# Decode attention over a long cache: K transposed in place by VectorE, scores by 512-column matmuls, 8 MB loads in three slots

## Chip, cores, metric

One core of a Trainium2 chip. The time is device microseconds (us) of one execution, as the median of several; the profile is one execution taken by the hardware profiler. The single runs of a kernel lie within some 0.2% of each other, and the median of the kernel before was 1311.9 to 1312.1 us in each of the four sets of runs, so differences of 1 us between medians can be read. All runs compared here are in the fast state; each run of an experiment shared its chip with runs of the kernel before. The changed kernel was measured in the first set only (1282.59 us).

## The reference

```python
def _A_ref(x, k_cache, v_cache, wq, wo):     # x (2,1,448); caches (2, 8, 32768, 256) bf16
    q = (x @ wq).reshape(B, Sq, 16, 256).transpose(0, 2, 1, 3)
    k = jnp.repeat(k_cache, 2, axis=1); v = jnp.repeat(v_cache, 2, axis=1)
    scores = jnp.einsum("bhqd,bhkd->bhqk", q, k) * (256 ** -0.5)
    o = jnp.einsum("bhqk,bhkd->bhqd", softmax(scores), v)
    return o.transpose(0, 2, 1, 3).reshape(B, Sq, 16 * 256) @ wo
# ... b = a small MLP with gelu, g = sigmoid((x * gate_w).sum(-1))
return g * a + (1 - g) * b
```

Two batches by 8 K/V heads are 16 groups. Each group has 32,768 positions of 256 values in K and as many in V, 16.8 MB each, so 537 MB must come from HBM for two query rows per group. There is next to no arithmetic per byte: this is a streaming kernel.

## The kernel before

K and V come in tiles of 4 MB (128 partitions, 64 positions each) through a ring of five slots. Each K tile is handled in 16 units. TensorE transposes a unit's eight 128x128 blocks into PSUM, ScalarE and VectorE take turns to copy them to SBUF, and TensorE multiplies each copied block with the two-column q.

```python
R, BR, NB = 64, 4, 5                       # positions per partition and tile, per unit; slots
def T(U):                                  # ... waits for the tile and for the eviction of U - 3
    for i in range(2 * BR):
        r, j = bl * BR + i // 2, i % 2
        e.transpose(bank[:, i * P:(i + 1) * P], kv[:, r, j * P:(j + 1) * P], ident_b[:, :])
def B(U):                                  # scores: K block as weights, q streams (2 columns)
    for i in range(BR):
        for j in range(2):
            e.matmul(pss[:, n, :], buf[:, (2*i+j)*P:(2*i+j+1)*P], qT_sb[:, kvh, j, :, b],
                     start=(j == 0), stop=(j == 1))
def C(v, bl):                              # values: two weights columns, V streams (256 columns)
    e.matmul(ps_o[g % 2][0:2, 0:Dh], pt[:, n, :], kv[:, r, :], start=..., stop=...)
# ... loads, on SyncE, in the order in which they are needed:
for d in seq:
    for pd in before_of[d]:
        E.wait("pe", released(pd))         # the slot's last user
    dma_start(view(d), src)
```

## Time and profile before

| | before |
|---|---|
| median time | 1311.9 us |
| instructions, matmuls | 44,891 and 21,141 |
| moved by DMA | 547.43 MB of data, 2.70 MB of instructions |
| mean rate | 420 GB/s over the span |

The prediction below shows the head of the page, the DMA queues and the stretches. Beside them stand the costliest groups of the page: the line, engine, operation and tiles, the count, busy us and mean ns of one, and the idle time before them with what ended most of it.

```profile
L513 ACT COPY KT<-psT 128x1024 bf16<-128x1024 bf16 x512 | 518.3, 1012 | 702.0 <-PE psT L374 700.2
L515 DVE COPY KT<-psT 128x1024 bf16<-128x1024 bf16 x512 | 354.1, 692 | 835.0 <-PE psT L374 835.0
L374 PE MATMUL psT<-ident_b,ring 128*128 128x128 bf16 x8192 | 556.2, 222 | 41.7 <-DMA ring<-in_A_k_cache_dram 38.3
...
L448 PE MATMUL ps_o<-ring,PT 128*2 128x256 bf16 x3840 | 496.3, 272 | 1.4 <-DMA ring<-in_A_v_cache_dram 1.4
...
L393 PE MATMUL ps_s<-qT_sb,KT 128*128 128x2 bf16 x8192 | 278.4, 163 | 1.2 <-issue 1.2
```

The two eviction groups wait for TensorE for 700 and 835 us, so they bind nothing. TensorE's transposes wait 38.3 us in total for K to land, in a span of 1310: TensorE and DMA are nearly even. The queue names matter later: q1 carries K, V and the weights, q8 and q14 carry instructions.

### The profile page before, as it was taken

What the parts mean: (1) busy time and instruction counts of PE and PEld (TensorE: products, weight loads), DVE (VectorE), ACT (ScalarE), POOL (GpSimd) and SP (SyncE); (2) the same over time, 40 slices, a digit from 0 to 9 for tenths busy, and PEclk for the clock granted to TensorE, in tenths of its full rate; (3) what the DMA queues carried; (4) which work ended last, traced back from release to release, by engine and by line L of the source; (5) the groups of instructions that cost most, each with busy time, mean ns of one, the idle gap of its engine ahead of it and who ended that gap; (6) DMA issues with size and microseconds to landing.
All of it is one profiled execution on the core that took longest, in us unless ns stands there. A gap on an engine that the chain in (4) does not pass through costs nothing.

```text
span 1310.5 us, 44891 instructions
## 1 busy us (share of the span) xinstructions
PE 1234.1 (94%) x21141; PEld 1031.1 (79%) x21141; DVE 388.7 (30%) x641; ACT 538.7 (41%) x597; POOL 1.5 (0%) x10
## 2 busy tenths in 40 slices
PE   4899999999999999999999999999999999999975
PEld 4888888888888787877787877878788778787864
DVE  2243332323332232323223232223232323223210
ACT  3364444444444444444444434444344434444410
POOL 0000000000000000000000000000000000000000
PEclk9699999999999999999999999999999999999986
DMA  9999999999999999999999999999999999999986
GB/s 392 433 424 418 431 428 429 428 426 429 428 430 430 427 430 427 428 430 429 428 428 427 426 423 424 422 429 416 419 420 429 422 428 415 430 423 421 430 344 294
DMA packets 22424, 550.30 MB, mean 420 GB/s; under 512 B 2392, under 2 KB 4576, under 8 KB 4704
## 3 DMA queue, kind: packets, MB, share of 16 engines
q1 hardware_dynamic: 22084, 547.43, 98.1%
q8 instruction: 165, 2.70, 0.8%
q14 instruction: 19, 0.16, 0.0%
q10 hardware_dynamic: 156, 0.01, 0.0%
HBM read 547.43 MB, written 0.00 MB: 418 GB/s over the span
## 4 chain that ended last, share of the span: by engine, by line
PE 53%; DMA 45%; SPq 1%; issue 0%; DVE 0%
DMA ring<-in_A_k_cache_dram 43%; PE psT L374 23%; PE ps_o L448 20%; PE ps_s L393 9%; DMA ring<-in_A_v_cache_dram 3%; SPq L314 0%; SPq L301 0%; PE ps_m L426 0%; PE ps_o L348 0%; PE ps_m L409 0%; PE ps_m L404 0%; PE ps_o L352 0%; PE ps_o L360 0%; PE psT L462 0%; PE ps_o L453 0%
## 5 line engine op out<-in xcount | busy, mean ns | idle before, releaser
L513 ACT COPY KT<-psT 128x1024 bf16<-128x1024 bf16 x512 | 518.3, 1012 | 702.0 <-PE psT L374 700.2
L515 DVE COPY KT<-psT 128x1024 bf16<-128x1024 bf16 x512 | 354.1, 692 | 835.0 <-PE psT L374 835.0
L374 PE MATMUL psT<-ident_b,ring 128*128 128x128 bf16 x8192 | 556.2, 222 | 41.7 <-DMA ring<-in_A_k_cache_dram 38.3
L374 PEld LDWEIGHTS psT<-ident_b,ring 128*128 128x128 bf16 x8192 | 468.0, 99 | 150.5 <-issue 97.7
L448 PE MATMUL ps_o<-ring,PT 128*2 128x256 bf16 x3840 | 496.3, 272 | 1.4 <-DMA ring<-in_A_v_cache_dram 1.4
L448 PEld LDWEIGHTS ps_o<-ring,PT 128*2 128x2 bf16 x3840 | 284.5, 83 | 85.1 <-DMA ring<-in_A_v_cache_dram 1.7
L393 PE MATMUL ps_s<-qT_sb,KT 128*128 128x2 bf16 x8192 | 278.4, 163 | 1.2 <-issue 1.2
L393 PEld LDWEIGHTS ps_s<-qT_sb,KT 128*128 128x128 bf16 x8192 | 259.9, 96 | 0.7 <-issue 0.7
L453 PE MATMUL ps_o<-PT,ring 128*128 128x2 bf16 x512 | 14.1, 164 | 16.9 <-DMA ring<-in_A_v_cache_dram 15.2
L453 PEld LDWEIGHTS ps_o<-PT,ring 128*128 128x128 bf16 x512 | 13.7, 101 | 17.5 <-DMA ring<-in_A_v_cache_dram 15.4
L543 ACT ACTIVATE PT<-ps_s,negm 128x256 bf16<-128x256 f32 x32 | 16.5, 543 | 0.5
L340 PE MATMUL ps_m<-xT,ring 128*128 128x2 bf16 x128 | 3.6, 165 | 9.4 <-DMA ring<-in_A_wq_dram 9.4
L627 DVE TENSOR_SCALAR o_sb<-ps_o,rl 2x256 f32<-2x256 f32 x15 | 7.1, 472 | 16.1 <-PE ps_o L448 16.1
L631 DVE TENSOR_TENSOR attnT<-ps_o,rl 128x2 bf16<-128x2 f32 x2 | 0.2, 158 | 37.9 <-PE ps_o L453 37.9
L604 DVE TENSOR_REDUCE mx<-ps_s 128x2 f32<-128x512 f32 x16 | 10.9, 681 | 1.3 <-PE ps_s L393 1.3
L340 PEld LDWEIGHTS ps_m<-xT,ring 128*128 128x128 bf16 x128 | 3.5, 104 | 9.4 <-issue 9.4
L426 PE MATMUL ps_m<-ident_f,o_sb 2*128 2x2 f32 x60 | 9.4, 258 | 0.6 <-DVE o_sb L627 0.6
L462 PE MATMUL psT<-ring,attnT 128*2 128x448 bf16 x32 | 9.1, 454 | 0.3 <-DVE attnT L631 0.3
L426 PEld LDWEIGHTS ps_m<-ident_f,o_sb 2*128 2x128 f32 x60 | 8.1, 191 | 1.1 <-DVE o_sb L627 0.9
L462 PEld LDWEIGHTS psT<-ring,attnT 128*2 128x2 bf16 x32 | 3.0, 99 | 5.2 <-issue 3.2
L404 PE MATMUL ps_m<-ident_f,mx 128*2 128x128 f32 x32 | 6.1, 272 | 0.0
L409 PE MATMUL ps_m<-diag,ones_f 2*128 2x2 f32 x32 | 6.1, 256 | 0.0
(54 smaller groups left out, 62.1 us busy)
## 6 DMA issues: line engine op xcount, KB each, us to landing
ring<-in_A_k_cache_dram SPq DMA_DIRECT2D x63, 4096.0 KB, 29.5
ring<-in_A_v_cache_dram SPq DMA_DIRECT2D x63, 4096.0 KB, 31.6
ring<-in_A_k_cache_dram SPq DMA_DIRECT2D x4, 1024.0 KB, 16.5
ring<-in_A_v_cache_dram SPq DMA_DIRECT2D x4, 1024.0 KB, 32.4
ring<-in_A_wo_dram SPq DMA_DIRECT2D x1, 3584.0 KB, 30.4
ring<-in_A_wq_dram SPq DMA_DIRECT2D x1, 3072.0 KB, 10.1
ring<-in_B_w_dram SPq DMA_DIRECT2D x1, 1568.0 KB, 35.3
ring<-in_B_w_dram SPq DMA_DIRECT2D x1, 1344.0 KB, 30.7
```

The lines of the kernel that those rows point to most:

```text
L340: E.ins(lambda e, w=w, xk=xk, kc=kc, kvh=kvh, j=j, hh=hh: e.matmul(ps_qT[:, kvh, j, hh, :], w, xk, start=(kc == 0), stop=(kc == KC)), key= ...
L374: E.ins(lambda e, bank=bank, i=i, kv=kv, r=r, j=j: e.transpose(bank[:, i * P:(i + 1) * P], kv[:, r, j * P:(j + 1) * P], ident_b[:, :]), ke ...
L393: E.ins(lambda e, pss=pss, n=n, i=i, j=j, buf=buf, kvh=kvh, b=b: e.matmul(pss[:, n, :], buf[:, (2 * i + j) * P:(2 * i + j + 1) * P], qT_sb ...
L426: E.ins(lambda e, j=j: e.matmul(ps_m[:, C_OT + 2 * j:C_OT + 2 * j + 2], o_sb[g % 2][0:2, j:Dh:2], ident_f[0:2, 0:2], start=True, stop=True ...
L448: E.ins(lambda e, g=g, kv=kv, r=r, n=n, pt=pt: e.matmul(ps_o[g % 2][0:2, 0:Dh], pt[:, n, :], kv[:, r, :], start=(n == 0), stop=(n == NT * ...
L453: E.ins(lambda e, g=g, kv=kv, r=r, n=n, j=j, pt=pt: e.matmul(ps_o[g % 2][:, 2 * j:2 * j + 2], kv[:, r, j:Dh:2], pt[:, n, :], start=(n == 0 ...
L462: E.ins(lambda e, c=c, kvh=kvh, hh=hh, j=j: e.matmul(ps_a, attnT[:, kvh, j, hh, :], wo_v[:, h, j * Dm:(j + 1) * Dm], start=(c == 0), stop= ...
L513: E.ins(lambda e: e.copy(buf[:, :], bank[:, :]), key=("E", U))
L515: E.ins(lambda e: e.tensor_copy(buf[:, :], bank[:, :]), key=("E", U))
L543: E.ins(lambda e, hh=hh: e.activation(PT[g % 2][:, :, hh], ps_s[g % 2][:, :, hh], ACTF.Exp, bias=negm[g % 2][:, hh:hh + 1], scale=SCALE, a ...
L604: E.ins(lambda e: e.tensor_reduce(mx[g % 2][:, :], ps_s[g % 2].rearrange("p n h -> p h n"), AX.X, ALU.max), key=("MX", g))
L627: E.ins(lambda e: e.tensor_scalar(o_sb[g % 2][:, :], ps_o[g % 2][0:2, 0:Dh], rl[g % 2][0:2, 0:1], None, op0=ALU.mult), key=("OS", g))
```

## The change

The intent is to take the transposes and the evictions off TensorE and PSUM. VectorE transposes K where it lies, in 32x32 blocks of 4-byte words (pairs of bf16). The transposed K then streams, 512 columns at a time, past weights in which q stands block-diagonally, and the scores of a whole group gather in one PSUM bank. V streams 512 columns at a time too, past four weight columns, in four column tiles of the array by turns. Loads become 8 MB in three slots.

```diff
-    R = 64
-    BR = 4
+    R = 128
+    CR = 16
-    NB = 5
+    NB = 3
+            def T(idx, blk):                                    # VectorE
+                if blk == 0:
+                    wait_fill(E, ("K", idx))
+                E.ins(lambda e: e.transpose(k_words(idx, blk), k_words(idx, blk)), key=("T", idx, blk))
+            def S(idx):                                         # TensorE, in place of T and B
+                for blk in range(NCK):
+                    E.wait("dve", ("T", idx, blk))
+                    for s in range(NS):
+                        e.matmul(pss, a_win(g, s, k), kv[:, blk * CR:(blk + 1) * CR, s // 2, :, s % 2],
+                                 start=(k == 0 and s == 0), stop=(k == NK - 1 and s == NS - 1))
+            def PV(v):                                          # TensorE, in place of C
+                for kk in range(0, NCK, 2):
+                    for r16 in range(CR):
+                        j = n % 4
+                        e.matmul(ps_o[g % 2][32 * j:32 * j + 4, :], pt[:, r16, k:k + 2, :], rows, ...)
+        for i in range(NTILES + LAG):                           # order of the loads; wo, last V at the end
+            order.append(("K", i)) ... order.append(("V", i - LAG))
+        order += [("WO", 0), ("V", LASTV)]
```

Cut: the weights' places in slot 0, q's copies, the softmax chain (now one maximum per row pair of 128 partial rows), and the last V tile, which comes in five pieces.

## The prediction

> **What bounds the kernel now.** I read the page first: parts 1 and 2, then the DMA queues (part 3), then the chain of waits (part 4).
>
> ```profile
> span 1310.5 us, 44891 instructions
> PE 1234.1 (94%) x21141; PEld 1031.1 (79%) x21141; DVE 388.7 (30%) x641; ACT 538.7 (41%) x597; POOL 1.5 (0%) x10
> ...
> DMA  9999999999999999999999999999999999999986
> ...
> q1 hardware_dynamic: 22084, 547.43, 98.1%
> q8 instruction: 165, 2.70, 0.8%
> ...
> PE 53%; DMA 45%; SPq 1%; issue 0%; DVE 0%
> ```
>
> Two things are full at once: PE is called 94% busy, and the 16 DMA engines are busy 98.1% of the span with the one queue that brings K, V and the weights. The chain names both (PE 53%, DMA 45%), so it doesn't settle which one binds. The table by stretches does. Its columns are the stretch, its length, busy time and instruction count of PE, PEld, DVE, ACT and POOL, the granted clock, the DMA share and GB/s.
>
> ```profile
> 0.00:10.00 10.00, 0.27 (x5) 0.21 (x5) 1.52 (x4) 1.60 (x3) 1.47 (x10) 1.00 0.81 318
> ...
> 200.00:400.00 200.00, 200.00 (x3396) 166.44 (x3393) 63.27 (x103) 88.80 (x100) 0.00 (x0) 1.00 1.00 429
> ...
> 800.00:1000.00 200.00, 192.33 (x3229) 159.59 (x3229) 59.73 (x97) 83.28 (x90) 0.00 (x0) 0.99 1.00 423
> ...
> 1240.00:1260.00 20.00, 20.00 (x304) 15.92 (x303) 5.62 (x11) 7.33 (x12) 0.00 (x0) 1.00 0.93 382
> 1260.00:1280.00 20.00, 10.91 (x196) 9.00 (x193) 0.72 (x4) 0.00 (x0) 0.00 (x0) 0.74 0.84 338
> ...
> 1300.00:1311.00 11.00, 5.26 (x128) 3.71 (x125) 0.90 (x3) 0.00 (x0) 0.00 (x0) 0.50 0.17 69
> ```
>
> From 20 to 1240 us the DMA share is 1.00: no DMA engine is idle. The rate is 423 to 429 GB/s there; the highest of any stretch I asked for was 435 (20 to 40 us). PE could go a little faster than that: in the timeline one pair of units (16 transposes, 16 score matmuls, 8 matmuls with V) repeats every 2.34 us and eats 1.049 MB, which is 448 GB/s. So **DMA binds, with PE some 5% behind it**. DMA loses time only at the two ends: the start, the stretch 1240 to 1280, and the end after the last landing. The DMA queue's own waits and the timeline say why the dip is there:
>
> ```profile
> SPq L314 <- PE ps_o L448: 664.3, 59, 21.1
> SPq L314 <- PE ps_s L393: 525.1, 62, 17.4
> ```
>
> ```profile
> 1253.50 14.51 SPq L314 DMA_DIRECT2D ring<-in_A_v_cache_dram  x2
> ...
> 1268.05 2.78 SPq L301 DMA_DIRECT2D ring<-in_A_v_cache_dram  x4
> ```
>
> The issuing engine waits for slots nearly always, which costs nothing while about three 4 MB loads are under way (29.5 us to landing against some 9.8 us for 4 MB). Near the end, the last V tile is issued only at 1268, when a slot comes free, and the DMA share falls to 0.84.
>
> [...]its packet records show 1213 ns as the median of a 32 KB packet, 27.0 GB/s on one engine, 432 on 16, and 309 ns for 8 KB; from the two, some 8 ns of a packet don't scale with size. [...]
>
> **The change, part by part.**
>
> *PE work removed.* Gone are 8192 transposes, 8192 two-column score matmuls that each load 128 columns, and 3840 V matmuls of 256 columns. They leave for 64 matmuls of 512 columns per 8 MB K tile (32 x 64 = 2048) and 64 of 512 columns per 8 MB V tile (30 x 64 = 1920, plus 2 x 256 = 512 two-column ones for the last group). With some 500 others that is about 5,000 matmuls in place of 21,141. The trace shows 8 V matmuls of 256 columns in 0.96 us, 120 ns each; doubling it, 512 columns should take about 0.22 to 0.24 us: 14 to 15 us per K tile, and 14 to 15 us per V tile if the four column tiles run one after another[...]. A K and a V tile together need 18 to 30 us of PE, against 39.3 us of DMA (16.78 MB at 427 GB/s). PE stops being a near-bound, but as it wasn't the bound, this alone is worth nothing in the middle.
>
> *VectorE work added.* 8 transposes per K tile of 128 x 2048 words: [...]18.3 us per K tile, 584 us in all. VectorE's 512 evictions (page, part 5: 354.1 us) and ScalarE's 512 (518.3 us) go. With softmax and closing work (some 4 us every second pair) VectorE is near 52% busy, inside the 39.3 us of a pair.
>
> *Do three slots of 8 MB feed the queue?* Load n+1 goes into the slot of load n-2 and must be issued before load n has landed, or DMA idles. Load n-2 landed two loads, 2 x 19.6 = 39 us, before load n. A K tile is held 18.3 us of transposes plus the last 8 matmuls, about 20 us. After the second K tile of a group PE must also pass the softmax chain (about 6 us, going by the 1254.7 to 1259.9 us of the timeline) before the V tile, which landed at 19.6, is used: released at 20 + 6 + (5 to 15) = 31 to 41 after the K tile's landing, 11 to 21 us after its own. Both are well below 39. So the queue always has the next load, and the middle stays at DMA's rate. At the start WQ, W1 and W2 share slot 0; K2 needs that slot back, wanted when K1 has landed (24.6 MB, about 57 us), while PE should be done with the weights by about 30 us. Hidden.
>
> *What DMA gains.* (a) The dip at 1240 to 1280: lost there against 427 GB/s are (45 x 20 + 89 x 20) / 427 = 6.3 us; in the packet records 5.1 us of it are idle engines. In the new order wo is issued when V29 is consumed (about 31 us after K31's landing, V30 being under way until 39), and the whole of the last V follows at once. I count 5.5 us won, and 1.5 us of new idling. (b) Instruction fetch: 165 packets of 16 KB at 1.05 us, 10.8 us of each engine's time, and they slow the K packet beside them from 1.2 to about 1.7 us (165 x 0.5 / 16 = 5 us); about 4 us of this overlap, so 11.7 us net. With about a quarter of the instructions left, some 8.5 us are won. (c) Half the completions (2,242 four-byte records, 1.3 us): 0.6 us. (d) If rows of 64 KB go as one packet, 8 ns x 8192 / 16 = 4 us; if split, nothing: 2 us. The start (0.81 share for 10 us) and the end (last landing at 1305.24, 5.3 us before the end: last matmuls, one more product, the store) stay within 0.5 us.
>
> Sum: 1311.9 - 5.5 + 1.5 - 8.5 - 0.6 - 2 - 0.5 = 1296.3; I take **1295 us**, 1.3% faster. The floor: 548 MB at 432 GB/s is 1269, plus 1.8 before the first byte, 5.3 at the end and 1.4 between span and measured time: 1277.
>
> **Rivals.** (1) *VectorE becomes the bound*: if 4-byte words transpose at half the rate, a block takes 4.4 us and a K tile 35. VectorE then does, per two pairs, 70 us of transposes and, in order, the softmax chain and the wait for the V tile that closes a group (20 to 25 us): over 90 against 78.6, some 1500 us. For it: no number for words anywhere in this trace. [...]I give it 5%. (2) *PE's new matmuls run slowly*: the score matmuls read K at a stride of 4 bytes, and PE, waiting in each V tile, may be granted half its clock (the page shows 0.50 to 0.74 in the waiting stretches at the end). At twice the time, K tiles cost 29 and V tiles up to 29: it would show first at wo, which could be issued after V30 has landed, and cost up to 15 us; with everything slow, a few per cent. (3) *All of the DMA losses vanish*: the slow packets (mean 1227 ns against 1213) were PE's and ScalarE's doing, and the rate rises to 431 or more: 1277 to 1285, just past 2%. Against it: they also come in stretches of equal work (429 against 423 GB/s), so they seem to belong to DMA itself. (4) *Nothing moves*: the transfers were hidden anyway, and a gap at each 8 MB hand-over takes back the gain: 1305 to 1312.
>
> **Range and chances.** The gains (a) to (d) are each bounded by a few us, so the middle of the distribution is narrow: 1286 to 1307. Faster by over 2% needs 1285.7 or less, which takes almost the whole of (3): 0.14. Slower needs (1), or (2) in full: 0.06. Within 2%: 0.80.
>
> **What would show it.** Right: DMA share 1.00 from 20 us to about 1290 without the dip; 426 to 431 GB/s; instruction queue below 0.8 MB; VectorE transposes near 2.28 us, 256 of them; VectorE near 50%, ScalarE below 5%; the chain almost all DMA; about 5,000 matmuls. Wrong: transposes over 4 us and DMA shares below 1 in every pair (rival 1); score matmuls over 0.4 us each (rival 2); a middle above 431 GB/s (rival 3); or waits of the issuing engine that end after the load before has landed, with GB/s dips every 20 us.

The 2.28 us for a block is an estimate. The trace of the kernel before has two reductions of 4-byte values on VectorE, 512 a partition in 681 ns (L604) and 128 in 278 (L609): 1.05 ns for each and some 144 ns fixed, by which 2048 would take 2.29 us if the transpose kept that rate, which this trace doesn't show. Nor does it show that the four column tiles overlap; the lower ends of 18 to 30 us and of 5 to 15 us suppose it.

## The result, and the profile after

| | before | after |
|---|---|---|
| median of the runs | 1311.93 us (1311.53 to 1312.07) | 1282.59 us (1282.37 to 1282.84) |
| ratio after to before | | 0.9777, 95% interval 0.9764 to 0.9791 |

A ratio is the mean time of one kernel's fast runs over that of the other's of the same rounds, so it is not quite the ratio of the medians. The change is faster by 2.2%, some 29.4 us; 1295 with a range of 1286 to 1307 was predicted. The direction was right, the size was little more than half of what came, and a gain of over 2% had been given a chance of 0.14 only.

The page of the kernel after, its head, DMA queues and the chain by engine:

```profile
span 1281.1 us, 10758 instructions
...
PE 742.5 (58%) x4977; PEld 306.7 (24%) x4977; DVE 621.8 (49%) x421; ACT 29.0 (2%) x118; POOL 3.5 (0%) x12
...
DMA  9999999999999999999999999999999999999997
...
DMA packets 12780, 548.12 MB, mean 428 GB/s; under 512 B 1336, under 2 KB 3520, under 8 KB 3904
...
q1 hardware_dynamic: 12580, 547.43, 99.1%
q8 instruction: 39, 0.64, 0.2%
...
DMA 60%; DVE 26%; PE 11%; ACT 1%; SPq 1%; issue 0%; another core or an unknown queue 0%; ACTq 0%
```

The data are the same 547.43 MB. Instructions fell to a quarter, the instruction queue q8 from 165 packets to 39, and the packets of data from 22,084 to 12,580. TensorE is at 58%, and 11% of the chain. (The chain also passes through VectorE, 26%, where the release of a slot ends last; but between 20 and 1200 us the packet records show hardly any idle time of the DMA engines, some 0.1 us in the mean of the 16, so nothing is lost there.) The stretches, with the columns that the prediction explains:

```profile
0.00:10.00 10.00, 0.27 (x5) 0.21 (x5) 4.08 (x9) 1.65 (x3) 3.45 (x12) 1.00 0.83 318
200.00:400.00 200.00, 120.04 (x700) 47.50 (x699) 103.09 (x71) 4.93 (x21) 0.00 (x0) 0.76 1.00 434
800.00:1000.00 200.00, 110.71 (x690) 43.65 (x685) 96.68 (x64) 4.92 (x21) 0.00 (x0) 0.78 1.00 433
1220.00:1240.00 20.00, 13.74 (x106) 5.71 (x104) 8.33 (x12) 0.95 (x3) 0.00 (x0) 0.91 0.96 409
1240.00:1260.00 20.00, 11.29 (x268) 8.43 (x269) 0.00 (x0) 0.00 (x0) 0.00 (x0) 0.53 1.01 394
```

The middle rose from 423 to 429 GB/s before to 432 to 434. The share was 1.00 in both kernels there: the engines were hardly ever idle (1.8 us of the 1220 before, in the mean of the 16), and yet they moved less before. The stretch 1220 to 1260 no longer holds a dip like the one of 0.84 and 338 GB/s.

The groups of the page that replace the five shown of before:

```profile
L385 PE MATMUL ps_s<-ring,Abd 128*128 128x512 bf16 x2048 | 529.7, 415 | 435.4 <-DVE ring L604 434.8
L604 DVE STREAM_TRANSPOSE ring<-ring 128x2048 uint32<-128x2048 uint32 x256 | 565.2, 2276 | 418.3 <-DMA ring<-in_A_k_cache_dram 418.3
...
L439 PE MATMUL ps_o<-ring,PT 128*4 128x512 bf16 x1920 | 138.4, 453 | 1.0 <-DMA ring<-in_A_v_cache_dram 1.0
```

VectorE's transpose takes 2276 ns, and 2.28 us had been expected. The mean of 415 ns in the line of the score matmuls is not what one costs, since they overlap: the timeline has eight of them in 1.91 us, 239 ns each. The 64 of a V tile take 3.6 to 6.2 us, down to 57 ns each against the 239: the four column tiles do run beside each other. The waits of the loading engine:

```profile
SPq L311 <- PE ps_s L385: 949.7, 31, 35.8
SPq L311 <- PE ps_o L439: 187.3, 29, 10.8
```

It waits for slots all the time, as before, and as before that costs nothing: V29 was released 29.2 us after K31 had landed (31 was forecast), with V30 still under way for another 10.

Three of the prediction's signs came out otherwise: the middle is above 431 GB/s (its sign of rival 3), the chain is DMA by 60% and not almost all, and the score matmuls show over 0.4 us in the page (its sign of rival 2, a false alarm, as just seen). The first is the one that matters. The question for the experiments is where 29 us came from when 15.6 had been counted.

### The profile page after: what moved, and what is told of

Its sections match the earlier page's. It is cut to its first block, busy times and chain, and to the rows that moved or that the text cites. A ratio compares the mean times of both kernels' runs of the same rounds, so it can differ in the third digit from the quotient of the medians.

```text
span 1281.1 us, 10758 instructions
## 1 busy us (share of the span) xinstructions
PE 742.5 (58%) x4977; PEld 306.7 (24%) x4977; DVE 621.8 (49%) x421; ACT 29.0 (2%) x118; POOL 3.5 (0%) x12
## 3 DMA queue, kind: packets, MB, share of 16 engines
q1 hardware_dynamic: 12580, 547.43, 99.1%
HBM read 547.43 MB, written 0.00 MB: 427 GB/s over the span
## 4 chain that ended last, share of the span: by engine, by line
DMA 60%; DVE 26%; PE 11%; ACT 1%; SPq 1%; issue 0%; another core or an unknown queue 0%; ACTq 0%
DMA ring<-in_A_k_cache_dram 58%; DVE ring L604 23%; PE ps_o L439 7%; PE ps_s L385 2%; DMA ring<-in_A_v_cache_dram 2%; ACT pexp L536 1%; DVE PT L623 1%; DVE mx L609 1%; SPq L306 1%; PE ps_m L406 1%; PE ps_m L396 0%; PE ps_m L401 0%; DVE gmax L611 0%; DVE gmx L617 0%; ACT negm L532 0%
## 5 line engine op out<-in xcount | busy, mean ns | idle before, releaser
L385 PE MATMUL ps_s<-ring,Abd 128*128 128x512 bf16 x2048 | 529.7, 415 | 435.4 <-DVE ring L604 434.8
L604 DVE STREAM_TRANSPOSE ring<-ring 128x2048 uint32<-128x2048 uint32 x256 | 565.2, 2276 | 418.3 <-DMA ring<-in_A_k_cache_dram 418.3
L385 PEld LDWEIGHTS ps_s<-ring,Abd 128*128 128x128 bf16 x2048 | 200.9, 103 | 758.2 <-DVE ring L604 347.3
L439 PE MATMUL ps_o<-ring,PT 128*4 128x512 bf16 x1920 | 138.4, 453 | 1.0 <-DMA ring<-in_A_v_cache_dram 1.0
L439 PEld LDWEIGHTS ps_o<-ring,PT 128*4 128x4 bf16 x1920 | 49.0, 97 | 82.0 <-issue 41.4
L609 DVE TENSOR_REDUCE mx<-ps_s 128x1 f32<-128x512 f32 x16 | 11.1, 692 | 32.2 <-PE ps_s L385 32.2
L415 PE MATMUL ps_m<-sel,o_sb 128*128 128x2 f32 x120 | 16.6, 260 | 12.0 <-DVE o_sb L638 12.0
L623 DVE STREAM_TRANSPOSE PT<-pexp 128x512 bf16<-128x512 bf16 x16 | 11.4, 711 | 23.7 <-ACT pexp L536 23.7
L415 PEld LDWEIGHTS ps_m<-sel,o_sb 128*128 128x128 f32 x120 | 15.3, 196 | 19.6 <-DVE o_sb L638 19.6
L458 PEld LDWEIGHTS ps_o<-PT,ring 128*128 128x128 bf16 x512 | 14.0, 103 | 15.5 <-DMA ring<-in_A_v_cache_dram 13.5
L527 ACT COPY Abd<-qrep 32x16 bf16<-32x16 bf16 x64 | 12.7, 199 | 0.6
```

What stands on the lines that cost most here:

```text
L385: E.ins(lambda e, g=g, s=s, k=k, kv=kv, blk=blk, pss=pss: e.matmul(pss, a_win(g, s, k), kv[:, blk * CR:(blk + 1) * CR, s // 2, :, s % 2], ...
L415: E.ins(lambda e, j=j, half=half: e.matmul(ps_m[:, C_OT + 2 * j:C_OT + 2 * j + 2], o_sb[:, half * Dh + j:(half + 1) * Dh:2], sel[:, 2 * ha ...
L439: E.ins(lambda e, g=g, j=j, rows=rows, pt=pt, r16=r16, k=t * NCK + kk, n=n: e.matmul(ps_o[g % 2][32 * j:32 * j + 4, :].rearrange("p (k d) ...
L458: E.ins(lambda e, g=g, kv=kv, r=r, k=k, r16=r16, j=j, pt=pt, t=t: e.matmul(ps_o[g % 2][:, 2 * j:2 * j + 2], kv[:, r, j:Dh:2], pt[:, r16, k ...
L527: E.ins(lambda e, o=o, Q=Q: e.copy(o, qrep[32 * Q:32 * Q + 32, :, kvh, :, b]), key=(("A", g) if Q == 3 else None))
L604: E.ins(lambda e: e.transpose(k_words(idx, blk), k_words(idx, blk)), key=("T", idx, blk))
```

## The experiments

The trace has one record for each DMA packet (start, duration, size, queue), but doesn't say which of the 16 DMA engines moved it. Summed up over the data queue and the instruction queue, per engine:

```
us per DMA engine                                     before    after
packets of K and V                                    1257.3   1241.7
packets of instructions (q8)                            10.8      2.6
time without a packet, mean of the 16 engines           11.0      4.0
first packet to the end of the last data packet       1302.9   1273.6
median packet of K and V                     1213 ns (32 KB)   2420 ns (64 KB)
```

Eleven runs test what these parts come from. The first four ask for the size of a packet, the fetch of instructions (two ways) and the stall at the end.

### 1. Packets of 32 KB again (`a_4mb`)

```diff
-    dma_start(cut(slot_of[d], 0, SLOT), src)
+    for h in range(2):                       # two halves of each row, one semaphore
+        dma_start(cut(slot_of[d], h * (SLOT // 2), SLOT // 2), src[:, h * (SLOT // 2):(h + 1) * (SLOT // 2)])
```

> The changed kernel (1282.6 us) with every 8 MB load cut into two of 4 MB, so that a packet is 32 KB again and there are twice as many completions; slots, engines and instructions stay. Theory A (size of the packet): each packet has about 8 ns that don't scale with its size, 8064 more packets over 16 engines are 4.0 us, and 1064 more completions 0.6 us: 1287 us, median packet 1213 ns. Theory B (load size matters by hand-over or by bunching of the engines at each load): the share of slow packets rises to that of the kernel before as well, another 3 to 4 us: 1291 us. Rival C (only the number of instructions and the stall at the end matter): 1282.6 to 1283.

Measured: 1287.21 us (ratio to before 0.9809, 0.9796 to 0.9823), 4.6 us over the changed kernel, and Theory A to the tenth. From the page of this run:

```profile
DMA packets 21853, 548.13 MB, mean 426 GB/s; under 512 B 2344, under 2 KB 4528, under 8 KB 4912
...
q8 instruction: 39, 0.64, 0.2%
```

The fetches are the changed kernel's 39 and the rest of its program is untouched, so **larger packets and fewer completions are worth 4.6 us**. The median packet was 1216 ns.

### 2. TensorE's instructions cut finer (`a_split`)

```diff
-    e.matmul(pss, a_win(g, s, k), kv[:, blk * CR:(blk + 1) * CR, s // 2, :, s % 2], ...)
+    for c in range(4):
+        e.matmul(pss[:, 4 * c:4 * c + 4, :], a_win(g, s, k), kv[:, blk * CR + 4 * c:blk * CR + 4 * c + 4, s // 2, :, s % 2], ...)
```

> The changed kernel with each score matmul of 512 columns cut into four of 128: 6144 more matmuls, each with its weight load, so about 12,300 more instructions on TensorE and 48 more fetches. Theory F: +5.3 us, 1287.9 us. If it is rather the busy TensorE than the fetches that slows DMA packets: more than that, with slow packets that don't stand beside a fetch. Rival none: 1282.6, as TensorE has room (58% busy).

Measured: 1291.89 us, +9.3. Busy time and the instruction queue:

```profile
PE 753.0 (58%) x11121; PEld 635.3 (49%) x11121; DVE 622.0 (48%) x421; ACT 29.0 (2%) x118; POOL 3.5 (0%) x12
...
q8 instruction: 87, 1.43, 0.4%
```

TensorE has the same 58% as in the changed kernel, the work is the same, and 48 more fetches cost 9.3 us, 0.194 us each. That is near twice Theory F's figure. About half of the loss stands in the packet records as idle engines in the last 100 us. So I looked at when each of the 16 engines finishes the same load: each writes a 4-byte completion record of its own (16 for each load in the records, 9 ns each). For the 61st K or V load, in us after the first of the 16:

```
changed kernel   0.0 0.3 0.5 0.7 0.8 0.9 1.0 4.1 |  6.1  6.2  6.3  6.4  7.0  7.1  7.7  8.2
a_split          0.0 0.4 0.5 0.6 0.8 0.9 1.0 3.9 | 15.5 15.6 15.7 15.7 15.7 16.0 16.0 16.5
```

**Eight engines run behind the other eight, and the lag grows with the fetches**: some 7 us with 39 fetches, 15.5 with 87. Early in both runs (9th load) all 16 lie within 3 to 4 us. If a fetch holds up one engine by about 1.5 us (1.05 for its own packet, 0.5 for the K packet beside it) and only eight engines serve them, 39 fetches are 39 x 1.5 / 8 = 7.3 us and 87 are 16.3. A load counts as landed with its last engine (the first of the 16 ends at 1198.9 us in both runs, the last at 1207.1 and at 1215.4, and the first transpose of this tile starts 0.5 us after the last, at 1207.6 and 1215.8), so the kernel's time follows the slower eight: 1.5 / 8 = 0.19 us for each fetch. I call this theory H; its rival S spreads the fetches over all 16, with 0.11 us each.

The packet records support theory H directly, although they don't name the engines. On one engine each packet starts some 4 ns before the one before it ends, so a fetch can be put in its place in the sequence. A fetch and the slower data packet after it take 1.55 us more than that data packet alone (median, in this run and in five others). From the 20th load on, 53 of the 55 fetches of `a_split` that could be followed, and all 23 of the changed kernel, stand on an engine that was among the slower nine at its completion before. And slow data packets that don't follow a fetch are rare here (19 against 10 in the changed kernel), so a busier TensorE is not what slows them.

### 3. Many instructions on GpSimd (`a_pool`)

```diff
+    for i in range(16000):                   # nothing waits for them
+        e.memset(dummy[0:1, i % 640:i % 640 + 1], 0)
```

> The changed kernel with 16,000 tiny memsets on GpSimd, which nothing waits for. It adds some 62 instruction fetches of 16 KB to the 39 of the changed kernel. Theory F (instruction fetches cost DMA time beyond their bytes: 13.8 us for 126 packets between the two kernels, 0.11 us each): +6.8 us, 1289.4 us, with the fetches near 100 packets. Rival bytes only (1.0 MB at 428 GB/s): +2.4 us, 1285. Rival none (fetches are hidden): 1282.6.

Measured: 1358.05 us, +75.5, a large miss. The stretches of this run with GpSimd at work and after it, and its two instruction queues:

```profile
400.00:600.00 200.00, 109.94 (x643) 43.85 (x645) 92.71 (x63) 4.93 (x21) 156.03 (x4664) 0.75 0.89 378
800.00:1000.00 200.00, 111.23 (x692) 44.12 (x694) 96.69 (x64) 4.92 (x21) 0.00 (x0) 0.78 1.00 429
```

```profile
q14 instruction: 130, 1.06, 0.2%
q8 instruction: 39, 0.64, 0.2%
```

The new fetches went through q14, not q8, in packets of 8 KB. The DMA share fell to 0.89 while GpSimd ran, and recovered when it had finished. The completions of one load (the 30th) showed 15 engines within 3.1 us and one 19 us behind. That suggests that q14's fetches all fall on one engine; but GpSimd's own traffic could have done it too, so this stayed open until run 7.

### 4. The kernel before without its stall at the end (`b_tail`)

```diff
+    wo_own = sb("wo_own", [P, NCH * Dm], dt.bfloat16)      # and small tiles shared to make room
+    if d == ("K", 32):
+        dma_start(wo_own, A_wo)                            # loaded half way through, not in a slot at the end
```

> The kernel before with wo in a tile of its own, loaded half way through, so that the last V tiles don't wait for a slot behind it. Theory T (the stall of the queue near the end is worth the idle engine time that the packet records show there, 6.9 us): 1311.9 - 5 to 7 = 1305 to 1307 us, and the dip of the DMA share before the end is gone. Rival: the stall is no loss, since the end is set by the last V tile's way through TensorE: 1310 to 1312.

Measured: 1312.03 us, ratio 0.9999 (0.9991 to 1.0007). Nothing. The end of this run by stretches:

```profile
1250.00:1260.00 10.00, 10.00 (x175) 8.41 (x173) 2.77 (x4) 4.20 (x5) 0.00 (x0) 1.00 1.01 431
...
1280.00:1290.00 10.00, 4.99 (x48) 2.29 (x45) 0.00 (x0) 0.00 (x0) 0.00 (x0) 0.51 0.81 345
1290.00:1300.00 10.00, 10.00 (x266) 7.78 (x265) 0.00 (x0) 0.00 (x0) 0.00 (x0) 0.84 0.49 204
```

The dip where the last V tile had waited is gone (431 GB/s), and one has come up 30 us later, at share 0.49, with all loads long issued: in the last 100 us of the data the engines idle for 9.6 us in the mean, against 8.8 before. The edit also made a dip of its own, where wo is loaded (0.84 and 332 GB/s at 600 to 620 us, 3.6 us of idle time). In all three dips, that of the kernel before at 1240 to 1280 us included, there are never fewer than eight engines with a packet, so the slower half never idles. Theory T falls. The idle time at the end was not a stall of the queue that could be won back: it was the faster engines having finished their part while the slower ones still worked. Whether they idle in front of the last load, behind it or half way is all the same. This is what theory H asks for.

### 5 and 6. The kernel before with fewer instructions (`b_half`, `b_few`)

Both are wrong on purpose (half of the sums is missing); loads, slots and packets stay.

```diff
# b_half
-    for j in range(2):                       # B: scores
+    for j in range(1, 2):
+    if r % 2 == 0: continue                  # C: every second V matmul
# b_few, as well
-    for i in range(2 * BR):                  # T: transposes; evictions of half the width
+    for i in range(1, 2 * BR, 2):
```

> The kernel before with half of its score matmuls and half of its V matmuls left out (wrong on purpose): 6016 matmuls less, so some 12,000 instructions and 47 fetches less; loads, slots and evictions stay. Theory H (0.19 us for each fetch, as the run with split score matmuls gave: 9.3 us for 48): 1312.1 - 9 = 1303 us. Theory S (fetches spread over 16 engines, 0.11 us each): -5.2, 1307. Rival TensorE (it was as much the bound as DMA): the 30% less TensorE work shows as more than that, 1295 or less. Rival none: 1311 to 1312.

> The kernel before with half of its transposes, score matmuls and V matmuls left out, and evictions of half the width (wrong on purpose): 10,112 matmuls less, some 20,200 instructions and 79 fetches less; loads and slots stay. Theory H (0.195 us for each fetch of TensorE's instructions, as 48 added and 47 removed ones gave): 1312.1 - 15.4 = 1296.7 us. If fetches mattered only up to a point, or if it was TensorE's time that the last run with removed matmuls won back, the next 32 fetches are worth little, since TensorE was already at 79%: 1301 to 1303.

Measured: 1302.67 and 1296.42 us, 9.5 and 15.6 us faster than the kernel before in the same rounds. Busy time and instruction queue of the first, then of the second:

```profile
PE 1027.8 (79%) x15125; PEld 845.4 (65%) x15125; DVE 387.3 (30%) x641; ACT 536.9 (41%) x597; POOL 1.5 (0%) x10
...
q8 instruction: 118, 1.93, 0.6%
```

```profile
PE 849.8 (66%) x11029; PEld 634.0 (49%) x11029; DVE 253.3 (20%) x641; ACT 318.9 (25%) x597; POOL 1.5 (0%) x10
...
q8 instruction: 86, 1.41, 0.4%
```

With 47 and 79 fetches less, a fetch is worth 0.201 and 0.198 us. Theory H had said 1303 and 1296.7; Theory S falls. TensorE's busy share went from 94% to 79% and 66%, and the second step won as much per fetch as the first (32 fetches, 6.3 us), as adding fetches had cost with TensorE at an unchanged 58%. **So it is the fetches and not the time of TensorE**. All runs by their fetches on q8:

```
packets of 64 KB:   39 fetches  1282.6      87 fetches  1291.9
packets of 32 KB:   39 fetches  1287.2 (a_4mb)   86  1296.4   118  1302.7   165  1312.0 (kernel before)
```

The second row is one line: with the 0.198 us of `b_few`, 126 fetches down from 1312.0 give 1287.1, and `a_4mb`, the changed kernel with the small packets, measured 1287.2. The count of eight shows in these runs as well: exactly eight engines have a packet for 12.7 us of the kernel before (165 fetches), 10.1 of `b_half`, 4.6 of `b_few` and 1.9 of `a_4mb` and of the changed kernel. The kernel before and the changed one differ in transposes, slots, evictions and order, and none of it is needed to explain the times.

### 7. Many instructions on ScalarE (`a_act`)

```diff
+    for c in range(300):                     # after each group; nothing waits for them
+        e.copy(dummy[0:1, c:c + 1], ident_b[0:1, 0:1])
```

> The changed kernel with 4800 tiny copies on ScalarE, 300 after each group, which nothing waits for. The run with 16,000 memsets on GpSimd lost 75 us, 63 of them with idle DMA engines, for 129 more fetches of 8 KB on the other instruction queue. Theory O (those fetches all fall on one single engine, 0.58 us each, and the other 15 wait for it): 4800 instructions are 37 fetches of 8 KB, +21 us if ScalarE's come through the same engine, 1304 us, with idle DMA engines. Rival G (the loss came from GpSimd itself[...]): 1282.6 to 1284 here.

Measured: 1302.79 us, +20.2. The instruction queues:

```profile
q8 instruction: 39, 0.64, 0.2%
q14 instruction: 43, 0.35, 0.1%
```

38 more packets on q14 for 4800 instructions (in run 3 it was 125 for 16,000, so one of 8 KB for some 128; on q8 it was 165 of 16 KB for the 42,282 of TensorE in the kernel before, one for 256) cost 20.2 us, 0.53 us each, as Theory O has it; Rival G falls, since GpSimd did nothing here. Completions of the 61st load, in us after the first:

```
a_act   0.0 0.0 0.1 0.2 0.2 0.6 0.8 1.0 1.1 1.3 1.5 1.5 1.5 1.8 2.1 | 17.9
```

One engine of 16 is 16 us behind the others, and for 11.4 us of this run exactly one engine has a packet. The same picture as with q8, with one engine in place of eight: each fetch costs the kernel about three times as much (2.7; 0.53 us here and 0.60 in run 3, against 0.198), though it is half as large. Whether it is the same engine for ScalarE's fetches and GpSimd's is not shown.

### 8. Bytes moved from eight engines to eight (`a_half8`)

```diff
-    dma_start(wo_v, wsrc)
+    for i in range(8):
+        dma_start(wo_v[8 * i:8 * i + 8], wsrc[8 * i:8 * i + 8])
+    dma_start(wo_v[64:P], wsrc[64:P])
```

> The changed kernel, with half of wo (1.8 MB) brought by eight DMAs of 8 partitions each[...]; the other half as before on all 16. New theory H: TensorE's instruction fetches are served by only 8 of the 16 engines; each costs some 1.5 us of one engine, so 39 fetches put that half 39 x 1.5 / 8 = 7.3 us behind, and a load counts as landed only with its slowest engine. Moving 1.8 MB to one half gives that half 4.2 us more and takes 4.2 us from the other. If the 8 chosen are the ones without fetches: 7.3 falls to 3.1 behind against 4.2: about 1279.5 us (-3.1). If they are the ones with fetches: +4.2, 1286.8 us. Rival S (fetches spread over all 16 engines, which are level): either way the chosen half falls 4.2 us behind: 1286.8. So only a faster time speaks against S; a slower one leaves both open.

Measured: 1308.78 us, +26.2: outside of every forecast, and my mistake in building it. The stretches of the new loads:

```profile
1240.00:1250.00 10.00, 0.00 (x0) 0.00 (x0) 0.00 (x0) 0.00 (x0) 0.00 (x0) 0.56 0.85 142
...
1260.00:1270.00 10.00, 1.58 (x55) 1.44 (x51) 0.00 (x0) 0.00 (x0) 0.00 (x0) 0.50 1.12 205
```

142 and 205 GB/s at shares of 0.85 and 1.12: the engines were busy and slow. A 1792-byte packet took 153 ns in the mean against 79 in the changed kernel. Each of the eight DMAs covered 8 neighbouring partitions; the next pair of runs is a control, in which eight DMAs on partitions 4 apart were not slowed (446 ns a packet, as in one DMA of all 128 partitions). Why these loads were slow is not shown, nor, by this run, that the eight DMAs kept to the same eight engines, which the forecast supposed. Of H it says nothing.

### 9 and 10. Extra bytes on eight engines, and on sixteen (`a_extra8`, `a_extra16`)

```diff
# early, into the part of slot 0 that the weights leave free; a_extra16: one DMA of all 128 partitions
+    for lo in (0, 32):
+        for i in range(lo, lo + 4):
+            dma_start(jd[i:lo + 32:4], js[i:lo + 32:4])     # partitions 4 apart
```

> The changed kernel with 0.75 MB of useless data loaded early, by eight DMAs of 8 partitions each[...]: 3.5 us more for each of these 8. Theory H (8 engines serve TensorE's fetches and end some 6.5 us behind the other 8): if the 8 chosen are the other ones, they have that much room and the time stays at 1282.6. If the 8 chosen are those with the fetches, or if all 16 are level: +3.5, 1286.1.

> The control of the last: the same early load for all 128 partitions in one DMA, 1.5 MB, 3.5 us more for each of the 16 engines. Every theory: +3.5 us, 1286.1.

Measured: 1285.51 us (+2.9) and 1285.68 us (+3.1). A packet of the extra load took 446 ns in both. By the expectation as written, that is no support for H: the eight engines chosen had no room. The completions show why. In us after the first, for the 2nd and the 61st load of `a_extra8`:

```
 2nd    0.0 0.0 0.1 0.2 0.3 0.6 1.0 2.1 | 3.3 3.4 3.5 3.6 3.7 4.0 4.3 5.2
61st    0.0 0.4 | 2.9 3.0 3.3 3.5 3.5 5.5 5.6 5.6 5.7 5.8 6.6 7.6 | 9.6 10.8
```

At the 2nd load eight engines are 3.3 us behind, so the eight DMAs did fall on eight of the 16, as built. At the 61st, two engines still lead, five stand where the other five leaders of the changed kernel would be with 3 us more, and two have moved on to 9.6 and 10.8. The records don't name the engines, so this is a reading and not shown: the eight chosen are a mixture, of which some serve fetches and most don't, the assumption that the eight would be all of one kind or all of the other was wrong, and the laggards that were also chosen set the end, +2.9. Which engines they are by number stays open.

### 11. Where VectorE would bind (`a_dve16`)

```diff
-    e.transpose(k_words(idx, blk), k_words(idx, blk))
+    for i in range(3 if blk % 2 else 1):     # three transposes are one
+        e.transpose(k_words(idx, blk), k_words(idx, blk))
```

> The changed kernel with every second 32x32 transpose done three times over (same result), 16 transposes per K tile in place of 8. By the arithmetic of the prediction's first rival: 16 x 2.28 = 36.5 us per K tile, 73 per two pairs, and in the same order on VectorE the softmax chain and the wait for the V tile that closes the group (11 us from the last transpose to the last product, going by the trace of the changed kernel, plus 2 us of trailing score matmuls): 86 us against 78 us of DMA: 16 x 86 = 1376 plus the 37 us before the first K tile and the 74 us after the last: about 1420 to 1450 us, VectorE above 80% busy. If VectorE's traffic to SBUF slowed DMA packets, the median packet would rise above 2.42 us; I expect that it does not. Rival: with 8 MB slots the holding time alone binds (a K tile held 38.5 us against a limit of 39) and it is 1290 to 1310.

Measured: 1489.8 us. (The sum in the expectation was added up wrongly: 1376 + 37 + 74 are 1487.) The busy line of the page and the transposes:

```profile
PE 875.7 (59%) x4977; PEld 329.0 (22%) x4977; DVE 1210.5 (81%) x677; ACT 29.0 (2%) x118; POOL 3.5 (0%) x12
...
L608 DVE STREAM_TRANSPOSE ring<-ring 128x2048 uint32<-128x2048 uint32 x512 | 1154.9, 2292 | 13.9 <-DMA ring<-in_A_k_cache_dram 5.1
```

The timeline repeats every 88.8 us per group, against 86 worked out. The rival by holding time alone falls. The median packet stayed (2418 ns against 2420), but the mean rose from 2424 to 2446 ns; what slowed those packets, in a run where DMA often waits, was not looked into. The changed kernel has room on VectorE, 49% busy, but not twice as much.

## Why the prediction was wrong

**Right.** DMA binds before and after (though by its slower half); the middle's share stays at 1.00; the slots never starve the queue; VectorE's cost per block (2276 ns), its share (49%), ScalarE's (2%), the count of matmuls (4977); TensorE's relief by itself is worth nothing. Of the rivals, (1) did not come, and `a_dve16` shows that its working was sound. (2) is visible, with the clock at 0.78 in the mean, and harmless, since TensorE is not on the path that sets the end.

**The step that failed is term (b)**, "Instruction fetch: [...] some 8.5 us are won". It divided the cost of a fetch by 16 engines, and took off 4 us as overlap. The runs show that TensorE's fetches fall on eight (the last eight completions of the 61st load come 6.1 to 8.2 us after the first with 39 fetches, 15.5 to 16.5 with 87), that the slower eight set the time, and that a fetch costs its engine the full 1.55 us. With 0.198 us of kernel time for each (the mean of 0.194, 0.201 and 0.198), 165 - 39 = 126 fetches are 24.9 us.

**Term (a)**, 5.5 us for the dip less 1.5 for new idling, was no gain of its own. `b_tail` took the stall away and won nothing. The idle time is the other side of the same lag, counted twice under two names.

**Terms (c) and (d)**, 0.6 and 2 us, together measured 4.6: the rows of 64 KB do go as one packet (2420 ns in the median).

The sum of what was measured is 24.9 + 4.6 = 29.5 us, and 29.4 were to be explained. The prediction's rival (3) named the right outcome and the wrong cause: it thought of slow packets made by the work of TensorE and ScalarE. Such packets exist: of the 433 of 32 KB in the kernel before that took over 40 ns more than the median, 320 don't follow a fetch, and the mean engine loses 8.7 us to them (0.3 in the changed kernel). But `b_tail` has 123 of them and 3.8 us, and the same time; so they did not set the time. What makes them is open. It was TensorE's fetches. I had their packets, and the slow ones beside them, in view, and averaged them over engines that don't share them evenly.

The lesson in reading: a share of 1.00 over 16 engines, with 423 to 429 GB/s where the median packet of 32 KB (1213 ns) makes 432 on 16 engines, looks like an even loss. (The prediction read that range too narrowly: its own table has 418 to 435 between 20 and 1240 us.) The place to look is not the mean, but the spread of the 16 completions of one load.

No run here beats the changed kernel. What the 39 fetches left still cost, some 7.7 us by the same slope, would need still fewer instructions on TensorE, and two streams of 268 MB in matmuls of 128 x 512 need some 4,000 matmuls in any case.

## What to carry to other kernels

When DMA binds a long unrolled kernel, its instructions are part of the traffic, and here their fetches fell on a part of the DMA engines only (with 39 fetches eight of 16 finish the 61st load 6.1 to 8.2 us after the first), so that each cost several times its bytes (0.198 us, where 16 KB at 428 GB/s are 0.04; the 165 of the kernel before come to some 33 us, an estimate from that slope): count instructions, prefer matmuls of 512 columns (cut into four of 128 they cost 9.3 us more), and keep chatter off the engines that have nothing to do (4800 tiny copies on ScalarE cost 20.2 us). Before you repair a stall at the end of a stream, check whether it is only the fast engines waiting for the slow ones: the repair in `b_tail` won nothing (1312.03 us). Rows of 64 KB in place of 32 were worth a few tenths of a per cent even at full rate (4.6 us of 1287).
